# A gated recurrence and a highway layer: another order of all operations, with the first load of f_logit ahead of the first of x

## The chip, the cores and the metric

The kernel runs on one core of a Trainium2 chip. The metric is the device time of one execution in microseconds (us); the times shown are medians of several executions. A profiled execution stands beside them: its own time, and the span that the profile covers, which is a little shorter. The engines are called PE (TensorE; PEld is its weight load), DVE (VectorE), ACT (ScalarE), POOL (GpSimd) and SP (SyncE, which issues the DMAs here).

## The reference

```python
sig = 1.0 / (1.0 + np.exp(-f_logit))                 # x, f_logit: 4 x 6336 x 256, float32
f = lower_bound + (1.0 - lower_bound) * sig
i = 1.0 - f
for t in range(S):                                   # S = 6336, for each of 4 sequences
    h = f[:, t] * h + i[:, t] * x[:, t]
    y[:, t] = h
# then, over all 25344 tokens of y
H = np.maximum(y @ w_h, 0.0)                         # w_h, w_t: 256 x 256
T = 1.0 / (1.0 + np.exp(-(y @ w_t + b_t)))
out = T * H + (1.0 - T) * y
```

## The kernel before

The 25344 tokens are cut into 29 units of 2, 2, 4, 4, 4, then 22 times 8, 4 and 2 blocks of 128 tokens (`parts`, L42). A unit is loaded with tokens on the partitions, turned so that the 256 channels lie on the partitions as two halves of 128, scanned along time, multiplied by both weights, and turned back by two matmuls that also add the parts of the result.

Every step of a unit is one token of the string `order` (L49): a letter, the unit, the half or piece, a `v` if the step runs on DVE instead of its usual engine, and behind the colon the number of its buffer. The tokens are issued in the order of the string, and `pin` keeps that order on each engine; nothing else plans the work. The letters are:

| token | what | engine | line |
|---|---|---|---|
| l, x | load of f_logit, of x (1024 KB for a unit of 8 blocks) | SP | L253 |
| u | u = sigmoid(-f_logit) | ACT | L265 |
| b | bv = u * x, by halves | POOL, or DVE with v | L273 |
| i, p | transposes of u and of bv | PE | L281, L301 |
| f | f = 1 - c * u from the transposed u | ACT, or DVE with v | L292, L290 |
| s | the scan along time, result y | DVE | L320 |
| z, g | the products with w_t and w_h | PE | L332, L112 |
| t | t = sigmoid(z + b_t) | ACT | L345 |
| d | d = max of -c * y and g (the weight w_h has one subtracted on its diagonal) | DVE | L349 |
| e | d * t, in pieces | POOL, or DVE with v | L355 |
| o | turned back, sum of c * y and d * t | PE | L377, L378 |
| c | copy from PSUM to SBUF | ACT, or DVE with v | L390, L388 |
| w | store | SP | L394 |

The two-letter tokens prepare constants once: wh and wt load the weights, pc and pb turn lower_bound and b_t, cc and cb store them, dg makes a diagonal matrix, IW subtracts one from the diagonal of w_h (POOL, L209), WHa and WTa scale the weights (ACT, L225). A token `k*N:slot` takes a PSUM buffer and fills it with N matmuls of zeros whose result nobody reads (`busy`, L120; L123 and L112 in the profile); with N = 0 it only takes the buffer. Three more zero matmuls (L151) always stand ahead of the string.

DVE and POOL products are tied by the helper `shared`: a POOL product waits for the last DVE product ahead of it in the string, if there is one that no POOL product has waited for yet.

There are six buffers for l and x each, eight for bv and y, four for u and f, three for t and d, five for the output, and in PSUM three double banks (slots 0 to 2) beside two single ones for transposes (a0 and a1, which other steps use too).

Of the kernel before, what the change touches and what calls it, by code (L numbers as in the profile page):

```python
# [61 lines left out]
c6.0:0 z8.1:1 i10.0:0 t8.1:2 s9.0:2 x11:5 f10.0v:0 e6.2 u11:3 g8.1:2 p9.1:1 z8.0:0 e7.2 i10.1:0 e7.0 l16:1 t8.0 g8.0:1 w3.0 o6.1:0
f10.1:2 d8.1:2 l12:2 s9.1:3 d8.0 e8.2v i11.0:0 k*2:2 u13:0 p10.1:1 s10.1:4 g9.1:2 c6.1:3 w5.1 w6.0 f11.0:1 e8.1 o7.0:1 c7.0:4 z9.0:0
l14:3 d9.1:1 t9.0:1 i13.1:0 p10.0:1 g9.0:1 f13.1:3 e8.0 s10.0:5 b11.0:6 z9.1:2 o7.1:0 p11.0:0 i11.1:1 d9.0 u12:1 b11.1:7 t9.1 o8.1:1
g10.0:2 f11.1:2 s11.0:0 d10.0:0 x12:0 c7.1:1 i12.1:1 w5.0 e9.0 x13:1 c8.1:0 u16:2 p11.1:0 f12.1v:0 b12.1:0 z10.0:0 t10.0:0 z10.1:1
o8.0:2 s11.1:1 t10.1 i12.0:1 b12.0:1 b13.0:3 l15:4 g10.1:0 f12.0:1 x14:2 w6.1 u14:3 i13.0:0 p12.1:1 w8.1 f13.0:2 c8.0v:2 x15:3 d10.1
g11.0:1 z11.0:2 z11.1:0 s12.1:6 d11.0:2 t11.0:2 p12.0:0 i14.0:1 b13.1:4 g11.1:2 k*1:1 o9.1:1 w7.0 t11.1 f14.0:0 p13.0:1 e10.0 s12.0:7
d11.1 o9.0:0 u15:1 w8.0 c9.1:3 i14.1:0 z12.0:2 f14.1:1 g12.1:1 x16:4 l18:5 i15.0:0 c9.0:0 s13.0:2 d12.1:1 b14.0:2 p13.1:1 o10.0:0
s13.1:3 w9.1 w7.1 f15.0:2 b14.1:5 b16.1:6 z12.1:1 t12.0:1 i16.0:0 l17:0 b15.0:7 o10.1:2 c10.0:4 t12.1 g13.0:0 c10.1:2 p14.0:1 z13.0:1
g12.0:2 f16.0:3 t13.0:0 e11.0v d13.0:0 s14.0:4 d12.0 z13.1:0 p14.1:0 w10.0 u18:0 l20:2 t13.1 s14.1:5 i15.1:1 f15.1:0 w9.0 w10.1 x17:5  # L70
o11.0:1 o11.1:2 b15.1:0 g13.1:0 e12.0 d13.1 p15.1:1 c11.1:3 i18.0:0 c11.0:1 s15.1:0 z14.0:2 f18.0:1 t14.0:2 z14.1:0 b16.0:1 t14.1
p15.0:0 o12.1:1 i16.1:1 g14.1:2 e13.0 o12.0:0 s15.0:1 d14.1:2 p16.0:0 u17:3 s16.0:6 l19:1 w11.1 f16.1:0 c12.1:4 c12.0:0 u20:1 g14.0:2
z15.1:1 d14.0 w11.0 x18:0 x19:1 t15.1:1 w12.1 i17.0:1 p16.1:0 s16.1:7 f17.0:2 g15.1:0 o13.1:2 o13.0:1 b17.0:3 i18.1:1 x20:2 d15.1:1
c13.1:2 p17.0:0 s17.0:2 c13.0:3 f18.1:3 z15.0:2 g15.0:0 l21:3 e14.0 b17.1:4 t15.0 i17.1:1 x21:3 d15.0 g16.0:1 z16.0:2 p17.1:0 d16.0:0
b18.1:2 f17.1:0 z16.1:0 u19:2 s17.1:3 g16.1:1 i19.0:1 b18.0:5 t16.0:0 d16.1 e15.0v t16.1 o14.0:2 f19.0:2 e16.0v c14.0:1 i19.1:0 o14.1:0
c14.1:4 z17.0:1 p18.0:1 w13.0 f19.1:0 w13.1 w12.0 s18.0:4 z17.1:2 b20.1:0 b19.0:7 b19.1:1 g17.1:0 t17.0:2 i20.0:0 t17.1 u21:3 o16.1:1
l22:4 p18.1:1 d17.1:2 g17.0:2 f20.0:1 o16.0:0 w14.0 b20.0:6 s18.1:5 c16.1:3 d17.0 l23:5 b21.1:3 i21.1:0 p19.0:1 f21.1:3 z18.0:1 k*0:2
p19.1:0 c16.0:2 s19.0:6 z18.1:2 o15.0:0 w16.1 t18.0:1 g18.1:1 t18.1 c15.0:0 x22:4 s19.1:7 e17.0 u22:0 p20.0:1 d18.1:0 o15.1:2 i21.0:0
g18.0:0 z19.0:1 s20.0:0 c15.1:1 f21.0:2 w16.0 d18.0 g19.0:2 d19.0:1 i20.1:1 p20.1:0 z19.1:0 t19.0:0 b21.0:4 f20.1:0 t19.1 o17.0:1
s20.1:1 e18.0 g19.1:2 l24:0 c17.0:3 d19.1 u23:2 b22.0:5 b22.1:2 o17.1:0 p21.0:1 i22.1:0 w17.0 w14.1 z20.1:1 s21.0:2 g20.1:2 f22.1:1  # L80
c17.1:2 p21.1:0 i22.0:1 t20.1:2 d20.1:2 f22.0:0 s21.1:3 o18.1:0 c18.1:3 o18.0:1 g20.0:2 p22.1:1 u24:1 x23:5 d20.0 s22.1:4 g21.0:0
i23.0:0 z21.0:2 c18.0:4 l28:2 e19.0 f23.0:2 w17.1 z20.0:1 i23.1:0 p22.0:1 d21.0:0 t21.0:1 f23.1:3 b23.1:7 w15.0 b23.0:1 l25:1 x24:0
t20.0 g21.1:2 e20.0 o19.0:0 u28:3 s22.0:5 i24.0:0 c19.0:2 o19.1:1 f24.0:1 p23.1:1 d21.1 w15.1 c19.1:0 z21.1:0 g22.1:2 s23.1:6 w18.1
t21.1 b24.0:6 z22.1:1 p23.0:0 o20.0:0 u25:0 d22.1:1 c20.0:1 t22.1:0 g22.0:2 s23.0:7 l26:3 i24.1:1 x25:1 o20.1:0 d22.0 p24.0:0 f24.1:0
b24.1:0 c20.1:3 z22.0:1 i25.0:1 t22.0 s24.0:0 g23.0:2 f25.0:3 w19.0 z23.1:0 p24.1:0 d23.0:2 g23.1:1 e21.0 o21.1:2 t23.1:2 b25.0:4
i25.1:1 u26:2 s24.1:1 o21.0:0 f25.1:2 c21.1:2 w20.0 p25.0:0 b25.1:3 x26:2 l27:4 d23.1 s25.0:2 c21.0:1 g24.1:1 w20.1 i28.1:1 z24.1:2
e23.2 e22.1 d24.1:0 z24.0:0 f28.1:1 p25.1:1 i26.0:0 w21.1 e22.0v t24.1:1 e22.2v e23.1v t24.0 f26.0:0 z23.0:2 s25.1:3 o22.0:1 b26.0:2
i28.0:0 o22.1:0 w18.0 t23.0 g24.0:2 f28.0:3 e23.0v c22.0:3 b26.1:5 e24.2 i26.1:0 w22.0 g25.0:1 d24.0 c22.1:2 u27:1 d25.0:1 f26.1:2
p26.0:1 o23.0:0 x27:3 z25.0:2 c23.0:4 w22.1 s26.0:4 e24.0 p26.1:0 w23.0 o23.1:1 z25.1:0 t25.0:0 c23.1:3 g25.1:2 t25.1 i27.0:1 s26.1:5
# [345 lines left out]
```

## Time and profile before

| | |
|---|---|
| median of 3 runs | 206.47 us (206.3 to 208.65) |
| profiled execution | 205.65 us, its span 203.9 us |
| busy, share of the span | PE 92%, DVE 94%, ACT 95%, POOL 85% |
| DMA | 78.68 MB, mean 386 GB/s |

A row of the table by stage gives a stretch of the span, its length, and the busy time of PE, PEld, DVE, ACT and POOL in it with the number of instructions, then TensorE's granted clock, the DMA engines' mean share and the GB/s. A row of a group by shape gives line, engine, operation, what is written and read, the count, the busy time in us, the mean of one in ns, and the idle time of the engine just ahead of them with what ended it. A row of the timeline gives start, length and the instruction, with the idle time ahead of it in brackets. A row of the chain of waits gives start, length and what the chain went through. A row of the waits gives who waited for whom: us in total, how often, the longest.

### The profile page before, as it was taken

The page shows a single profiled execution, that of the slowest core. Times are in us where ns is not written, and L with a number is a line of the kernel's source. Part 1 is how long each engine was busy: PE and PEld are TensorE (multiplying, and loading weights), DVE is VectorE, ACT ScalarE, POOL GpSimd, SP SyncE. Part 2 cuts the span into 40 slices and gives each one's busy share as a digit, 9 for nine tenths or more (in the row PEclk, how much of TensorE's full clock was granted, in tenths as well). Part 3 has the DMA queues.
Part 4 walks back from the last instruction along what each step waited for, and adds up shares of the span by engine and source line. Part 5 has one row for each costly group of instructions (what it writes and reads, how often), then busy time and mean ns, then how long its engine had stood idle before and what let it go on. Part 6 is the DMA issues. An engine that isn't in the chain of part 4 may idle for free.

```text
span 203.9 us, 4594 instructions
## 1 busy us (share of the span) xinstructions
PE 187.5 (92%) x1794; PEld 131.9 (65%) x1820; DVE 192.6 (94%) x162; ACT 194.2 (95%) x203; POOL 172.8 (85%) x96
## 2 busy tenths in 40 slices
...
GB/s 213 367 420 424 416 418 423 409 420 422 418 426 416 423 424 417 420 419 424 417 423 420 427 416 416 427 419 273 336 341 411 420 416 399 209 289 367 272 372 251
DMA packets 16413, 78.68 MB, mean 386 GB/s; under 512 B 1796, under 2 KB 2568, under 8 KB 10760
## 3 DMA queue, kind: packets, MB, share of 16 engines
...
q10 hardware_dynamic: 8, 0.00, 0.0%
...
## 4 chain that ended last, share of the span: by engine, by line
PE 47%; POOL 13%; ACT 12%; DMA 11%; DVE 7%; issue 5%; SPq 1%; ACTq 0%; POOLq 0%; DVEq 0%
DMA x<-in_x_dram 11%; POOL bv L273 8%; PE op L377 7%; PE op L378 7%; PE z L332 6%; PE g L332 6%; PE uT L281 6%; POOL d L355 6%; PE bT L301 5%; DVE y L320 5%; PE z L112 5%; PE g L112 5%; ACT o L390 4%; ACT t L345 3%; ACT f L292 3%
## 5 line engine op out<-in xcount | busy, mean ns | idle before, releaser
L273 POOL TENSOR_TENSOR bv<-u,x 128x1024 bf16<-128x1024 f16 (+2 forms) x53 | 103.7, 1981 | 15.9 <-DVE d L355 7.7
L320 DVE TENSOR_TENSOR_SCAN y<-f,y,bT 128x1024 bf16<-128x1024 f16 (+5 forms) x56 | 107.4, 1929 | 1.1 <-ACT f L292 0.9
L355 POOL TENSOR_TENSOR d<-d,t 128x512 bf16<-128x512 bf16 (+3 forms) x30 | 68.1, 2279 | 6.3 <-ACT t L345 3.6
L349 DVE SCALAR_TENSOR_TENSOR d<-y,ncc,g 128x1024 bf16<-128x1024 bf16 (+2 forms) x58 | 63.6, 1107 | 0.4 <-issue 0.2
L345 ACT ACTIVATE t<-z,bt 128x1024 bf16<-128x1024 f32 (+2 forms) x58 | 58.5, 1048 | 0.5 <-PE z L112 0.5
L292 ACT ACTIVATE f<-uT,ncc 128x1024 f16<-128x1024 f16 (+2 forms) x55 | 58.1, 1060 | 0.5 <-PE uT L281 0.2
L390 ACT COPY o<-op 128x1024 f32<-128x1024 f32 (+2 forms) x55 | 50.9, 966 | 2.1 <-PE op L378 1.8
L265 ACT ACTIVATE u<-l 128x2048 f16<-128x2048 f32 (+2 forms) x29 | 50.4, 1736 | 1.8 <-DMA l<-in_f_logit_dram 1.7
L378 PE MATMUL op<-ident_b,d 128*128 128x128 bf16 x396 | 49.7, 219 | 1.2 <-DVE d L355 0.9
L377 PE MATMUL op<-diag,y 128*128 128x128 f16 x396 | 50.0, 219 | 0.8 <-DVE d L349 0.3
L378 PEld LDWEIGHTS <-d 128*128 128x128 bf16 x396 | 44.0, 113 | 5.5 <-issue 1.3
L377 PEld LDWEIGHTS <-y 128*128 128x128 bf16 x396 | 44.2, 113 | 2.4
L332 PE MATMUL z<-y,w_sb 128*128 128x512 bf16 (+1 forms) x116 | 39.7, 368 | 0.7 <-DVE d L349 0.2
L332 PE MATMUL g<-y,w_sb 128*128 128x512 bf16 (+1 forms) x112 | 39.3, 367 | 1.0 <-DVE d L349 0.2
L301 PE MATMUL bT<-ident_f,bv 128*128 128x128 f32 x198 | 31.9, 277 | 4.8 <-POOL bv L273 2.3
L281 PE MATMUL uT<-ident_h,u 128*128 128x128 f16 x396 | 31.5, 219 | 2.9 <-DVE y L320 1.5
L281 PEld LDWEIGHTS <-u 128*128 128x128 f16 x396 | 26.5, 98 | 11.8 <-issue 4.7
L332 PEld LDWEIGHTS <-w_sb 128*128 128x128 f16 x232 | 22.2, 98 | 14.8 <-ACT f L292 0.2
L301 PEld LDWEIGHTS bT<-ident_f,bv 128*128 128x128 f32 x198 | 22.6, 141 | 14.1 <-POOL bv L273 5.8
L112 PE MATMUL z<-y,w_sb 128*128 128x512 bf16 x79 | 29.9, 379 | 0.0
L112 PE MATMUL g<-y,w_sb 128*128 128x512 bf16 x76 | 28.8, 379 | 0.1
L112 PEld LDWEIGHTS <-w_sb 128*128 128x128 f16 x176 | 17.2, 98 | 15.2 <-issue 1.4
...
## 6 DMA issues: line engine op xcount, KB each, us to landing
...
x<-in_x_dram SPq DMA_DIRECT2D x22, 1024.0 KB, 15.0
...
out_dram<-o SPq DMA_DIRECT2D x2, 256.0 KB, 15.0
```

What stands on the lines that cost most here:

```text
L112: return pe.add_instruction(mybir.InstMatmult(name=nc.get_next_instruction_name(), start_tensor_calc=start, stop_tensor_calc=stop, tile_si ...
L273: shared(pin(e.tensor_mul(bv[:, :nb // 2].rearrange("p k d j -> p k j d"), st[n]["u"][:, :nb, own].rearrange("p (k j) d -> p k j d", j=2), ...
L281: pin(nc.tensor.transpose(uT[:, j * P:(j + 1) * P], st[n]["u"][:, j, h * P:(h + 1) * P], ident_h))
L292: pin(nc.scalar.activation(to, of, AF.Identity, scale=ncc[:, h:h + 1], bias=1.0))
L301: pin(nc.tensor.transpose(words[:, k:k + g * (P - 1) + 1:g], pair, ident_f))
L320: pin(nc.vector.tensor_tensor_scan(y[:, c:e], st[n]["f", h][:, c:e], st[n]["bT", h][:, c:e], 0.0 if fresh else carry[h], op0=ALU.mult, op1 ...
L332: pin(nc.tensor.matmul(p[:, a:e], w, half(n, "y", ki)[:, a:e], start=ki == 0, stop=ki == NH - 1))
L345: pin(nc.scalar.activation(half(n, "t", m), st[n]["z", m][:, :tokens(n)], AF.Sigmoid, bias=bt[:, m:m + 1]))
L349: pin(nc.vector.scalar_tensor_tensor(half(n, "d", m), half(n, "y", m), ncc[:, m:m + 1], st[n]["g", m][:, :tokens(n)], op0=ALU.mult, op1=AL ...
L355: shared(pin(e.tensor_mul(st[n]["d"][:, a:c], st[n]["d"][:, a:c], st[n]["t"][:, a:c])), not eng)
L377: pin(nc.tensor.matmul(o, half(n, "y", h)[:, cols], diag[:, h], start=True, stop=False))
L378: pin(nc.tensor.matmul(o, half(n, "d", h)[:, cols], ident_b, start=False, stop=True))
```

## The change

Only the string `order` is replaced. Both strings have 850 tokens and the same units, pieces and loads; what differs is their order, the buffers' numbers, which of the b, f, e and c run on DVE, and the fillers. The first load is now l0, ahead of x0. Loads of the start, before: x0 l0 l1 wh x1 l2 wt x2 l3 x3; after: l0 x0 l1 wh x1 wt l2 x2 l3 x3. The fillers by tokens are 21 matmuls of zeros before and 15 after.

On DVE before: b0.1 b0.0 b1.1 b1.0 b2.1; f1.0 f10.0 f12.1; e0.1 e0.0 e1.1 e1.0 e2.0 e3.1 e4.0 e6.0 e6.1 e8.2 e11.0 e15.0 e16.0 e22.0 e22.2 e23.1 e23.0 e24.1 e25.1 e26.2 e26.0 e27.1 e27.0 e28.0; c8.0 c27.1. On DVE after: b0.1 b2.0; f0.1 f1.1 f6.1 f8.0 f17.1; e2.0 e6.0 e7.0 e9.0 e8.0 e13.0 e16.0 e19.0 e23.0 e22.0 e25.0 e26.0 e26.2 e27.1 e28.0 e28.1; c27.0 c28.0 c28.1.

The beginning and the end of both strings (the rest, as far as the counts go, is summed up above):

```diff
-k*3:a0 x0:0 pc:0 l0:0 l1:1 cc u0:0 k*3:1 pb:2 i0.0:1 k*4:0 dg wh u1:1 b0.1v:0 f0.0:0 b0.0v:1 i1.0:0 x1:1 l2:2 wt IW f1.0v:1 p0.0:1 WHa
-cb i0.1:0 s0.0:0 f0.1:2 x2:2 b1.1v:2 b1.0v:3 k*2:1 i1.1:1 k*1:0 p0.1:0 f1.1:3 p1.0:1 s0.1:1 k*1:2 p1.1:0 l3:3 g0.0:1 s1.0:2 g0.1:0 u2:2
-s1.1:3 x3:3 k*1:2 i2.1:1 d0.1:0 l4:4 WTa d0.0 g1.0:2 i2.0:0 g1.1:0 z1.1:1 b2.1v:4 f2.1:0 d1.1:1 d1.0 f2.0:2 p2.1:1 s2.1:4 b2.0:5 t1.1:0
-z0.0:1 z0.1:0 z1.0:2 u3:3 x4:4 t0.1:1 t1.0 t0.0 l5:5 x5:5 p2.0:0 b3.1:6 i3.1:1 f3.1:1 s2.0:5 e0.1v e0.0v e1.1v k*3:0 i3.0:0 g2.0:2 l6:0
-u4:0 e1.0v x6:0 b3.0:7 z2.0:1 b4.0:1 f3.0:3 p3.1:1 t2.0:2 d2.0:2 g2.1:0 i4.1:0 o0.0:2 z2.1:1 f4.1:0 s3.1:6 b4.1:0 d2.1 c0.0:0 t2.1
-p3.0:1 i4.0:0 f4.0:2 s3.0:7 e2.0v p4.0:0 l7:1 z3.1:2 x7:1 p4.1:1 o1.0:0 s4.0:0 u5:1 c1.0:1 s4.1:1 z3.0:1 i5.1:0 g3.1:0 e2.1 t3.0:1
-g4.1:1 d3.1:0 i5.0:1 g3.0:0 d4.1:1 b5.1:3 b5.0:2 f5.1:1 t3.1 p5.1:0 l8:2 f5.0:3 z4.0:2 z4.1:1 u6:2 t4.0:0 p5.0:1 d3.0 o2.0:0 l9:3
-s5.1:2 t4.1 s5.0:3 e3.0 c2.0:2 b6.1:4 i6.1:0 b6.0:5 g4.0:2 f6.1:2 e4.1 u7:3 p6.1:1 z5.1:1 i6.0:0 d4.0 z5.0:0 s6.1:4 g5.0:2 t5.1:2
-f6.0:0 p6.0:1 i7.0:0 x8:2 l10:4 e3.1v e4.0v g5.1:1 d5.0:2 o4.0:2 w1.0 s6.0:5 i7.1:1 t5.0 b7.0:6 x9:3 d5.1 f7.0:1 u8:0 c4.0:3 p7.0:0
-e5.0 s7.0:0 g6.0:0 b7.1:7 f7.1:3 g6.1:1 d6.1:1 p7.1:1 e5.2 i8.1:0 u9:1 x10:4 z6.0:2 f8.1:2 t6.0:1 z6.1:1 t6.1 i8.0:0 o3.0:2 f8.0:0
-b8.1:1 s7.1:1 u10:2 g7.0:1 b8.0:0 p8.0:1 d6.0 l11:5 e6.0v e6.1v w2.0 i9.0:0 d7.0:0 o5.1:0 w0.0 c3.0:4 b9.0:3 s8.0:6 e5.1 z7.1:1 f9.0:1
-b10.1:2 g7.1:2 p8.1:0 i9.1:1 l13:0 b9.1:4 t7.1:0 c5.1:1 z7.0:1 d7.1 f9.1:3 w4.0 o5.0:2 e7.1 p9.0:1 o6.0:0 s8.1:7 b10.0:5 t7.0 c5.0:2
 ...
-w24.0 c25.2 o25.1:2 z27.1:1 c25.0:1 p28.0:1 g27.1:a0 t27.1:1 c25.1 b28.1:0 e26.2v e26.0v e26.1 o26.2:0 s28.0:0 z27.0:1 w25.1 d27.1:0
-p28.1:1 o26.3:2 c26.2:2 g27.0:a0 o26.1:0 s28.1:1 t27.0 e27.1v c26.3 g28.1:1 d27.0 c26.1:0 o26.0:2 e27.0v z28.1:a1 z28.0:0 c26.0
-o27.1:a0 d28.1:1 w25.0 o27.0:1 w26.1 c27.1v:4 w26.0 g28.0:2 t28.0:0 t28.1 e28.1 d28.0 e28.0v o28.1:a1 c27.0 w27.0 c28.1:3 o28.0:a0
-w28.1 c28.0:1 w28.0
+l0:0 k*3:a0 k*0:0 pc:1 k*0:2 u0:0 i0.0:1 x0:0 l1:1 cc wh i0.1:0 b0.1v:0 x1:1 b0.0:1 dg f0.0:0 p0.1:1 f0.1v:1 IW u1:1 b1.1:2 s0.1:0 WHa
+k*2:0 p0.0:0 wt s0.0:1 k*4:2 i1.1:1 pb:1 WTa f1.1v:2 l2:2 k*0:0 g0.0:2 i1.0:0 f1.0:3 x2:2 g0.1:0 p1.1:1 d0.0:0 l3:3 b1.0:3 p1.0:0 d0.1
+z0.0:2 z0.1:0 u2:2 cb s1.1:2 t0.0:0 k*1:1 s1.0:3 b2.0v:4 i2.0:1 x3:3 i2.1:0 f2.0:1 b2.1:5 g1.0:1 e0.0 t0.1 f2.1:0 p2.0:1 s2.0:4 z1.1:2
+z1.0:0 p2.1:0 l4:4 u3:3 x4:4 b3.0:6 s2.1:5 e0.1 b3.1:7 l5:5 d1.0:1 k*2:a1 t1.1:1 g1.1:2 d1.1 t1.0 i3.0:1 f3.0:2 p3.0:0 x5:5 z2.0:0
+s3.0:6 i3.1:1 u4:0 z2.1:1 g2.0:2 f3.1:3 t2.1:2 i4.1:0 p3.1:1 b4.1:0 d2.0:2 f4.1:1 o0.0:1 g2.1:2 i4.0:0 t2.0 l6:0 e1.0 s3.1:7 b4.0:1
+p4.1:1 u5:1 d2.1 z3.1:0 g3.0:2 s4.1:0 f4.0:0 p4.0:1 e1.1 i5.0:0 t3.1:0 x6:0 c0.0:0 d3.0:0 o1.0:2 l7:1 e2.1 b5.0:2 s4.0:1 g3.1:0 d3.1
+i5.1:1 g4.0:1 f5.0:2 e2.0v b5.1:3 d4.0:1 z3.0:0 c1.0:1 f5.1:3 t3.0 p5.0:0 x7:1 l9:2 o2.0:2 k*1:1 u6:2 c2.0:2 s5.0:2 g4.1:0 p5.1:1
+s5.1:3 i6.0:0 z4.0:1 f6.0:1 e3.1 l8:3 d4.1 t4.0:1 w0.0 z4.1:2 i6.1:0 t4.1 b6.1:4 p6.1:1 z5.1:1 x8:2 g5.1:0 l10:4 f6.1v:0 u7:3 t5.1:2
+i7.0:0 f7.0:2 b6.0:5 s6.1:4 z5.0:2 k*1:1 x9:3 d5.1:2 l11:5 w1.0 p6.0:1 i7.1:0 e3.0 e4.1 t5.0 b7.1:6 e5.2 f7.1:3 u9:0 s6.0:5 g5.0:1
+p7.1:0 o3.0:0 i9.0:1 z6.0:2 d5.0 b7.0:7 g6.1:1 c3.0:3 e4.0 f9.0:0 s7.1:6 d6.1:0 u8:1 p7.0:1 g6.0:0 i8.1:0 e5.0 t6.0:0 o4.0:1 s7.0:7
+f8.1:1 o5.1:2 i8.0:0 d6.0 l12:0 f8.0v:3 i9.1:1 e5.1 b8.1:0 g7.1:0 u10:2 c5.1:4 c4.0:0 p8.1:0 f9.1:2 x12:4 b8.0:1 z6.1:2 g7.0:1 t6.1
+b9.0:2 p8.0:1 u11:3 o5.0:2 d7.1:1 c5.0:1 b9.1:3 s8.1:0 z7.1:0 i11.0:0 x10:5 s8.0:1 d7.0 t7.1:1 e6.2 p9.0:1 w2.0 w5.1 f11.0:1 s9.0:2
 ...
+t26.1:0 g26.0:1 c24.0:3 w24.1 t26.0 b28.0:6 o25.3:2 b28.1:1 w21.0 d26.0 e26.0v c25.3:1 o25.2:a0 i28.1:1 e26.2v c25.2 f28.1:1 w22.1
+o25.0:0 o25.1:2 c25.0:0 z27.1:a0 p28.0:1 e26.1 s28.0:0 g27.0:1 z27.0:0 d27.0:0 c25.1 t27.1:2 o26.3:2 w24.0 p28.1:1 s28.1:1 g27.1:a0
+o26.2:1 d27.1 t27.0 o26.1:0 c26.3:4 c26.2 e27.0 w25.1 e27.1v c26.1:2 g28.0:2 o26.0:a1 w25.0 c26.0 z28.0:1 o27.0:a0 z28.1:0 d28.0:1
+t28.0:1 w26.1 o27.1:2 g28.1:1 c27.0v:3 e28.0v t28.1 d28.1 w26.0 e28.1v o28.0:0 c28.0v:1 o28.1:a1 c27.1 c28.1v:0 w27.0 w28.0 w28.1
```

More of the change, by code (lines that the diff above doesn't have):

```diff
@@ L62 @@
[L62 to L89, printed above, removed]
@@ L90 @@
-d25.1 e25.0 o24.1:1 e24.1v g26.1:0 i27.1:0 d26.1:2 b27.0:7 g26.0:2 c24.1:2 f27.1:0 b27.1:1 z26.1:1 x28:4 d26.0 f27.0:2 p27.0:0 w23.1
-z26.0:0 t26.1:2 w21.0 e25.2 w24.1 o24.0:2 p27.1:1 o25.3:1 s27.0:6 e25.1v o25.2:a0 t26.0 b28.0:6 s27.1:7 c24.0:4 o25.0:0 c25.3:3 w19.1
-w24.0 c25.2 o25.1:2 z27.1:1 c25.0:1 p28.0:1 g27.1:a0 t27.1:1 c25.1 b28.1:0 e26.2v e26.0v e26.1 o26.2:0 s28.0:0 z27.0:1 w25.1 d27.1:0
-p28.1:1 o26.3:2 c26.2:2 g27.0:a0 o26.1:0 s28.1:1 t27.0 e27.1v c26.3 g28.1:1 d27.0 c26.1:0 o26.0:2 e27.0v z28.1:a1 z28.0:0 c26.0
@@ new lines @@
+b9.0:2 p8.0:1 u11:3 o5.0:2 d7.1:1 c5.0:1 b9.1:3 s8.1:0 z7.1:0 i11.0:0 x10:5 s8.0:1 d7.0 t7.1:1 e6.2 p9.0:1 w2.0 w5.1 f11.0:1 s9.0:2
+e7.2 e6.1 l13:1 z7.0:2 t7.0 e6.0v b10.0:4 z8.0:0 b10.1:5 t8.0:2 i10.0:0 z8.1:1 t8.1 p9.1:1 o6.1:2 g8.0:0 x11:0 e7.0v f10.0:3 w4.0
+g8.1:1 w5.0 c6.1:2 p10.0:0 s9.1:3 u12:1 i10.1:1 x13:1 f10.1:0 d8.1:2 b12.1:6 d8.0 o6.0:2 s10.0:4 c6.0:4 z9.0:1 e7.1 g9.1:0 l14:2
+b11.1:7 b11.0:0 p10.1:1 d9.1:0 w3.0 s10.1:5 u13:0 t9.0:0 b12.0:1 o7.1:2 i11.1:0 o7.0:0 w6.0 f11.1:2 c7.0:0 g9.0:1 d9.0 i12.0:0 c7.1:1
@@ new lines @@
+p11.1:1 z9.1:0 f12.0:3 s11.1:6 z10.0:2 t9.1 i12.1:0 e9.0v z10.1:1 e8.0v i13.1:1 w6.1 t10.0:1 g10.0:0 e8.1 t10.1 f13.1:0 d10.0:1 g10.1:2
+f12.1:2 o9.0:1 e8.2 b13.1:2 d10.1 p11.0:1 o8.0:0 p12.1:0 c9.0:3 x14:2 l18:3 e10.0 o8.1:2 u14:2 l15:4 w7.1 s11.0:7 s12.1:0 g11.1:1
+c8.1:4 c8.0:2 i13.0:1 b13.0:3 w7.0 w9.0 b14.1:4 f13.0:1 z11.1:2 p12.0:0 t11.1:0 d11.1:2 b14.0:5 g11.0:0 i14.1:1 o9.1:1 s12.0:1 z11.0:2
+u18:3 p13.1:0 d11.0 f14.1:2 p13.0:1 t11.0 s13.1:2 z12.0:0 x15:3 c9.1:1 t12.0:2 o10.0:2 z12.1:1 l16:5 c10.0:0 u15:1 w8.0 w8.1 g12.1:0
```

22 lines of the change are left out of this document (added).

## The prediction

> **What bounds the kernel now.** I read the page's totals first, then the table by stage, then the chain of waits, then the timelines of the first 50 us, then the groups kept apart by shape.
>
> ```profile
> span 203.9 us, 4594 instructions
> PE 187.5 (92%) x1794; PEld 131.9 (65%) x1820; DVE 192.6 (94%) x162; ACT 194.2 (95%) x203; POOL 172.8 (85%) x96
> 0.00:20.00 20.00, 16.19 (x102) 8.71 (x104) 15.05 (x32) 16.32 (x28) 8.21 (x18) 1.00 0.92 354
> 20.00:60.00 40.00, 35.80 (x341) 24.91 (x345) 39.21 (x31) 39.86 (x38) 37.34 (x22) 1.00 1.02 419
> ...
> 140.00:180.00 40.00, 39.35 (x398) 28.57 (x402) 39.69 (x28) 40.00 (x40) 37.93 (x16) 1.00 0.87 339
> 180.00:204.00 24.00, 19.13 (x215) 14.63 (x215) 18.93 (x23) 18.09 (x27) 13.12 (x11) 0.97 0.84 320
> ```
>
> Columns of the stage rows: length, busy time of PE, PEld, DVE, ACT, POOL, granted clock, DMA share, GB/s. From 20 to 180 us DVE and ACT have no idle time to speak of (39.21 and 39.86 of 40, then 39.69 and 40.00), and until 140 us DMA is full as well. The idle time that an order could win back lies at the two ends: 5.0 us of DVE and 3.7 us of ACT before 20 us, 5.1 and 5.9 us after 180 us. Even all of DVE's idle time, 203.9 - 192.6 = 11.3 us, is only 5.5% of the span, and the first load's latency and the last store keep most of it.
>
> ```profile
> 0.74 0.38 SPq L253 DMA_DIRECT2D x<-in_x_dram  x1
> 1.18 0.90 SPq L253 DMA_DIRECT2D l<-in_f_logit_dram  x2
> 4.13 0.63 ACT L265 ACTIVATE u<-l 128x512 f16<-128x512 f32 x1 [1.29 <-DMA l<-in_f_logit_dram]
> 10.59 16.55 DMA x<-in_x_dram
> 27.28 2.15 POOL bv L273
> 30.23 2.35 DVE y L320
> ```
>
> The first three rows are the timeline: x0 is issued at 0.74 us, l0 at 1.18, and u0 starts at 4.13 when l0 is there. The other three are the chain of waits: to 27.1 us (10.59 + 16.55) it runs through an x transfer, then through POOL's product of u and x (by POOL's list, in which IW, b2.0, b3.1, b3.0, b4.0, b4.1, e2.1, b5.1, b5.0 and e3.0 come first, this is b6.1, so the transfer is x6), then through the scan of unit 6. So the start is bound by the load stream, not by what the engines do with it, and from 30 us on by DVE and ACT, with POOL close behind.
>
> **The change part by part.** Both orders hold the same 850 tokens but for slots, fillers and engines, so the work can be counted. Engines first: durations by shape.
>
> ```profile
> L273 POOL TENSOR_TENSOR bv<-u,x 128x1024 bf16<-128x1024 f16 x44 | 94.4, 2169 | 7.8 <-DVE d L355 5.1 <-ACT t L345 1.4 <-DMA x<-in_x_dram 0.8
> L273 POOL TENSOR_TENSOR bv<-u,x 128x512 bf16<-128x512 f16 x7 | 8.0, 1167 | 7.6 <-DVE bv L273 5.0 <-DVE d L355 2.1 <-DMA x<-in_x_dram 0.4
> L273 POOL TENSOR_TENSOR bv<-u,x 128x256 bf16<-128x256 f16 x2 | 1.3, 687 | 0.5 <-DVE d L355 0.5
> L273 DVE TENSOR_TENSOR bv<-u,x 128x256 bf16<-128x256 f16 x4 | 1.5, 439 | 0.0
> L355 POOL TENSOR_TENSOR d<-d,t 128x2048 bf16<-128x2048 bf16 x10 | 40.8, 4078 | 0.3 <-POOL bv L273 0.3
> L355 POOL TENSOR_TENSOR d<-d,t 128x1024 bf16<-128x1024 bf16 x5 | 10.6, 2137 | 0.0
> L355 POOL TENSOR_TENSOR d<-d,t 128x512 bf16<-128x512 bf16 x14 | 16.1, 1159 | 2.4 <-DVE d L355 2.4
> L355 POOL TENSOR_TENSOR d<-d,t 128x256 bf16<-128x256 bf16 x1 | 0.7, 667 | 3.6 <-ACT t L345 3.6
> L355 DVE TENSOR_TENSOR d<-d,t 128x2048 bf16<-128x2048 bf16 x3 | 3.6, 1215 | 0.0
> L355 DVE TENSOR_TENSOR d<-d,t 128x1024 bf16<-128x1024 bf16 x4 | 2.7, 681 | 0.1
> L355 DVE TENSOR_TENSOR d<-d,t 128x512 bf16<-128x512 bf16 x12 | 4.9, 426 | 0.1
> L355 DVE TENSOR_TENSOR d<-d,t 128x256 bf16<-128x256 bf16 x5 | 1.2, 282 | 0.1
> L209 POOL TENSOR_TENSOR w_raw<-w_raw,ident_f 128x128 f32<-128x128 f32 x2 | 0.9, 453 | 3.5 <-DMA w_raw<-in_moe_w_h_dram 3.5
> L290 DVE TENSOR_SCALAR f<-uT,ncc 128x1024 f16<-128x1024 f16 x2 | 2.5, 1267 | 0.0
> L290 DVE TENSOR_SCALAR f<-uT,ncc 128x256 f16<-128x256 f16 x1 | 0.5, 485 | 0.8 <-PE uT L281 0.8
> L292 ACT ACTIVATE f<-uT,ncc 128x1024 f16<-128x1024 f16 x42 | 50.4, 1200 | 0.0
> L390 ACT COPY o<-op 128x1024 f32<-128x1024 f32 x42 | 44.2, 1091 | 0.9 <-PE op L378 0.8
> L390 ACT COPY o<-op 128x256 f32<-128x256 f32 x2 | 0.6, 375 | 0.9 <-PE op L378 0.9
> L388 DVE COPY o<-op 128x1024 f32<-128x1024 f32 x1 | 1.2, 1194 | 0.0
> ```
>
> *DVE.* Three b of 256 leave it: -1.32. Its e go from 24 (5, 12, 4, 3 of 256, 512, 1024, 2048) to 16 (2, 3, 7, 4): 12.89 to 11.47, -1.42. Its f go from two of 1024 and one of 256 to three and two: +1.75. Of its copies one of 1024 and one of 512 become one of 512 and two of 256; a copy of 256 on DVE isn't shown, so I take ACT's 0.375 (bounds 0 and 1.194): -0.44. Sum -1.4 us.
> *ACT.* One f of 1024 and one of 256 less (the latter at DVE's 0.485; ACT's own lies between that and nothing shorter is shown), one copy of 1024 more, two of 256 less: -1.20 - 0.49 + 1.09 - 0.75 = -1.35 us.
> *POOL.* Three b of 256 more (+2.06); its e go from 30 (1, 14, 5, 10) to 38 (4, 23, 2, 9): 68.4 to 70.3. Sum +4.0 us, to about 177 of 204.
> *PE.* Fifteen zero matmuls by slots instead of 21; PE's idle time is not on the chain at either end, so 0.
>
> So the two full engines each lose about 1.4 us over the whole run. How much of it reaches the end depends on where it lies, and there the x6 transfer cuts the run in two.
>
> *Before x6 (to 27.3 us).* With l0 ahead of x0, l0 is issued 0.44 us earlier (1.18 - 0.74) and u0 can start that much earlier; bounds 0 (l0's latency may not shrink) and 1.29 (ACT's whole wait). wt moves ahead of l2, which puts 256 KB before l2 (0.6 us at 419 GB/s); x2 keeps its place. But up to x6 stand the same transfers in both orders: x0 to x6, l0 to l6 and both weights (256 KB each for units 0 and 1 and the weights, 512 for 2 to 4, 1024 for 5 and 6: 8.9 MB). So x6 lands at 27.1 us again, and the 0.44 us ends in the wait for it. What it costs if that cover is gone: up to 0.44 us gained.
>
> What can go wrong there is POOL. Before b6.1 its list now has 17 operations instead of 10 (b0.0, b1.1, b1.0, e0.0, e0.1, e1.0, e1.1 are the new ones): 18.1 us instead of 13.4 by the rows above (IW is the two at L209). The first four fit into the time when it idled (the first row below: 5.05 us). From b2.1 on, which can start at about 11.5 us as POOL's first b did at 11.66, 15.2 us remain; operations overlap a little, and the window's row below has 17.03 us busy for nine operations of 17.47 us by their means, so 14.8: POOL is through at 26.3 us, 1.0 us ahead of x6, if it waits for nothing. It will wait: for x3 as now, and for e2.0 on DVE, which stands ahead of b5.1 (the helper `shared` lets a POOL operation wait for the DVE product before it).
>
> ```profile
> POOL bv L273 <- DVE d L355: 7.7, 7, 2.6
> POOL d L355 <- DVE d L355: 2.4, 3, 1.0
> 27.28:45.06 17.78, 14.77 (x126) 9.46 (x126) 17.02 (x12) 17.64 (x16) 17.03 (x9) 1.00 1.01 417
> 11.66 1.17 POOL L273 TENSOR_TENSOR bv<-u,x 128x512 bf16<-128x512 f16 x1 [5.05 <-DVE bv L273]
> 40.80 4.26 POOL L273 TENSOR_TENSOR bv<-u,x 128x1024 bf16<-128x1024 f16 x2
> 47.21 2.34 DVE L320 TENSOR_TENSOR_SCAN y<-f,y,bT 128x1024 bf16<-128x1024 f16 x1
> ```
>
> Ten such waits took 10.1 us, 1.0 each. With 1.0 for e2.0 and 0.4 for x3 (the row of b of 512), b6.1 starts at 27.7 instead of 27.3: **+0.4 us**; bounds 0 (no wait) and +1.5 (the 2.1 + 0.4 us that the b of 512 waited).
>
> *Units 6 to 8.* From b6.1 to the end of b8 POOL had nine operations, 17.47 us by their means; now it has twelve (e3.0, e4.0 and e5.1 are added), 20.95, and times 17.03/17.47 that is 20.4 us. From 27.3 the last b8 would end at 47.7 and the one ahead of it at 45.6 us. Between the end of b6.1 (29.43) and its scan (30.23) lie 0.8 us of transposes, so s8.1 could start at 46.4. DVE, by its own list, has four products less from s6.1 up to there (e3.1, e4.0 and e6.1 of 512, e6.0 of 1024: 1.96) and f8.0 more (1.27); that stretch took 47.21 - 30.23 = 16.98 and now takes 16.3, so DVE is there at 46.5. That fits with nothing to spare, where the old order had b8 done at 45.06, 2.2 us ahead of its first scan. Bounds of the wait: 0 and 3.5 (all of POOL's added work); nearest to 0, because no DVE product stands inside this list, but with no slack I take **+0.3 us**.
>
> *From the first scan of unit 6 to the end* DVE has 0.7 us less. Of its -1.4 us, the other 0.7 lie ahead of s6.1: three b and four e of 256 and f1.0 gone (1.32 + 1.13 + 0.49), f0.1, f1.1 and f6.1 added (0.97 + 1.27). **-0.7 us.** POOL then gains slack again, because the new order gives DVE whole products of 2048 or pieces of 1024 from unit 6 on. The load order later keeps or lengthens the distance from issue to use, so no new DMA wait: 0. At the tail the last product, the last two copies and three stores follow each other in the same way, both copies on DVE instead of ACT: 0, bounds -0.3 (one copy's 0.375) and +0.4.
>
> Sum: +0.4 + 0.3 - 0.7 = 0.0 us. The profiled execution took 205.65 us with a span of 203.9; the median of the runs shown is 206.47. I take 0.1 off for the 0.44 us at the start (a quarter of it) and forecast **206.3 us**, a span of about 203.8.
>
> **The rivals.**
> *A. POOL becomes the bound and it ends slower.* If b6.1 starts 1.5 us late and POOL waits in units 6 to 11 as much as it did between 20 and 60 us, where it idled 40 - 37.34 = 2.66 us, then with no slack all of it reaches DVE: 1.5 + 2.66 - 0.7 = +3.5, some 209.8 us. It decides when POOL's idle time between 12 and 50 us is over about 1.5 us. For it: the +8.2 us of POOL work up to b8 (18.1 + 20.95 against 13.4 + 17.47). Against: three DVE products ahead of b8 instead of twelve, so fewer of the 1.0 us waits. Two such waits more and it passes 210.6.
> *B. The lighter engines gain.* If x6 isn't what holds b6.1 (its transfer may land sooner where the stream starts smoother), DVE's and ACT's 1.4 us and the 0.44 us count in full and nothing is lost at unit 8: -1.8, 204.6 us. For it: ACT, 40.00 of 40, gets 1.35 us less. Against: x6 has the same bytes ahead.
> *C. PE runs slow at first.* The new order has no filler between lbT's transpose and the first transposes of u.
>
> ```profile
> 1.19 1.46 PE L151 MATMUL idle<-zeros 128*128 128x512 bf16 x3 [1.19 <-DVE zeros L148]
> 4.41 0.59 PE L112 MATMUL idle<-zeros 128*128 128x512 bf16 x2
> ```
>
> Three zero matmuls took 1.46 us at the start, two took 0.59 at 4.41: the pace doubles at about 4 us. If it stays slow some us longer, each of the four groups in a row ahead of e0 (transposes of u and b, g, z) costs 0.49 - 0.30 = 0.19 us more, 0.8 in all; POOL reaches b6.1 that much later, and the time is 207.1. [...]
> *D. The start doesn't move:* u0 waits for something other than its place in the queue, and the 0.1 goes: 206.4.
>
> **How the numbers follow.** Forecast with D: 0.50 (205.3 to 207.3). A: 0.27, of it 0.11 beyond 210.6. B: 0.16, of it 0.05 beyond -2% (202.3), where the tail's 5 us of idle time would have to shrink as well. C: 0.07. A measurement of this kernel tells about 2%, 4.1 us, from no change. So faster 0.05, same 0.84, slower 0.11. The range leaves out the upper end of A and the lower end of B: 203.9 to 210.2.
>
> **What would show it.** Right: b6.1 at 27 to 28 us after a wait for x; u0 at 3.7; DVE over 39 of 40 from 20 to 60 us with POOL over 38.5. Wrong: gaps of DVE in front of scans of units 6 to 11 that end with POOL's b (A); x6 landing before 26 us, or DVE under 190.5 us busy with no new idle time (B); zero matmuls still at 0.42 us apart after 5 us (C). It would be wrong as a whole if a wait deep in the new order (a scan behind its f on ACT, a store that holds a load) cost more than any at the start, which the counts can't exclude.

## The result: 0.7% slower, and where the time went

The changed kernel took 208.36 us (median of 20 executions, 205.66 to 211.5), the kernel before 206.47 us (20 executions, 205.82 to 208.65). The ratio is 1.0071 with a 95% interval of 1.0049 to 1.0094; it isn't the quotient of the two medians, since disturbed executions, some 3 to 4 us longer, are left out of it and of the ratios below. The profiled execution took 208.23 us, its span 206.4.

First the totals of the changed kernel's page, then its table by stage (length; busy PE, PEld, DVE, ACT, POOL; granted clock, DMA share, GB/s). Its `order` has one line less, so every line number is smaller by one: L354 is now the product e.

```profile
span 206.4 us, 4642 instructions
PE 190.2 (92%) x1814; PEld 131.5 (64%) x1814; DVE 195.1 (95%) x154; ACT 193.8 (94%) x200; POOL 177.3 (86%) x107
```

```profile
0.00:20.00 20.00, 16.66 (x97) 8.87 (x98) 13.31 (x25) 15.09 (x25) 12.17 (x25) 1.00 0.93 354
20.00:60.00 40.00, 36.48 (x333) 23.94 (x332) 39.60 (x30) 40.00 (x39) 38.32 (x24) 1.00 1.01 417
...
140.00:180.00 40.00, 38.42 (x383) 27.48 (x382) 40.00 (x28) 39.18 (x38) 36.42 (x16) 1.00 0.89 360
180.00:204.00 24.00, 22.32 (x244) 16.55 (x241) 22.52 (x25) 20.60 (x30) 16.72 (x14) 1.00 0.71 272
```

Two things catch the eye. DVE was busy for only 13.31 of the first 20 us instead of 15.05, which is a larger drop than the 0.7 us by which its list ahead of unit 6 had been counted lighter; and over the whole run it was busy for 195.1 us instead of 192.6, though 1.4 us had been taken from it. The groups by shape say which product grew, and the timelines of DVE and POOL say why.

```profile
L354 DVE TENSOR_TENSOR d<-d,t 128x2048 bf16<-128x2048 bf16 x4 | 8.2, 2044 | 0.0
L354 DVE TENSOR_TENSOR d<-d,t 128x1024 bf16<-128x1024 bf16 x7 | 4.6, 679 | 0.1
```

```profile
106.60 2.95 DVE L354 TENSOR_TENSOR d<-d,t 128x2048 bf16<-128x2048 bf16 x1
130.07 1.20 DVE L354 TENSOR_TENSOR d<-d,t 128x2048 bf16<-128x2048 bf16 x1
148.38 2.83 DVE L354 TENSOR_TENSOR d<-d,t 128x2048 bf16<-128x2048 bf16 x1
```

```profile
100.00 8.47 POOL L272 TENSOR_TENSOR bv<-u,x 128x1024 bf16<-128x1024 f16 x4
109.72 2.17 POOL L272 TENSOR_TENSOR bv<-u,x 128x1024 bf16<-128x1024 f16 x1 [1.25 <-DVE d L354]
...
143.74 11.59 POOL L272 TENSOR_TENSOR bv<-u,x 128x1024 bf16<-128x1024 f16 x5
```

The mean of a DVE product of 2048 went from 1215 to 2044 ns, that of 1024 stayed at 0.68 us. Two of the four took 1.20 us and two far longer: e13.0 (106.60) and e19.0 (148.38). When e13.0 was issued, the last of POOL's four b ran until 108.47 (100.00 + 8.47), and e13.0 ended 1.08 us after that. So it was not computing for 2.95 us: b17.0 still took 1.87 us when e13.0 was issued, and e13.0 took 1.75 us longer than the 1.20 us of an undisturbed one. e19.0 came 0.4 us after the start of b22.0 and took about 1.6 us longer. In the kernel before, by contrast, POOL had reached its wait when DVE came to its large products:

```profile
120.30 2.36 DVE L355 TENSOR_TENSOR d<-d,t 128x2048 bf16<-128x2048 bf16 x2
122.79 10.60 POOL L273 TENSOR_TENSOR bv<-u,x 128x1024 bf16<-128x1024 f16 x5 [2.62 <-DVE d L355]
```

There two products took 2.36 us together, and POOL paid with 2.62 us of idle time. POOL loses time at an overlap as well: five of its products took 10.60 us there, and 11.59 us from 143.74 on in the changed kernel, where b22.1, issued while e19.0 was at work, took 3.15 us instead of 2.2.

The other loss is at the start (first ACT's row of u1 in the kernel before, then rows of ACT, PE, DVE and POOL in the changed kernel):

```profile
4.95 0.63 ACT L265 ACTIVATE u<-l 128x512 f16<-128x512 f32 x1 [0.19 <-DMA l<-in_f_logit_dram]
...
3.57 0.63 ACT L264 ACTIVATE u<-l 128x512 f16<-128x512 f32 x1 [0.71 <-DMA l<-in_f_logit_dram]
5.99 0.63 ACT L264 ACTIVATE u<-l 128x512 f16<-128x512 f32 x1 [0.83 <-DMA l<-in_f_logit_dram]
6.98 1.49 PE L111 MATMUL idle<-zeros 128*128 128x512 bf16 x3
8.71 0.48 DVE L289 TENSOR_SCALAR f<-uT,ncc 128x256 f16<-128x256 f16 x1 [1.17 <-PE uT L280]
12.75 1.28 DVE L319 TENSOR_TENSOR_SCAN y<-f,y,bT 128x512 bf16<-128x512 f16 x1 [0.71 <-PE bT L300]
27.61 4.25 POOL L272 TENSOR_TENSOR bv<-u,x 128x1024 bf16<-128x1024 f16 x2
31.76 2.35 DVE L319 TENSOR_TENSOR_SCAN y<-f,y,bT 128x1024 bf16<-128x1024 f16 x1
47.95 4.58 DVE L319 TENSOR_TENSOR_SCAN y<-f,y,bT 128x1024 bf16<-128x1024 f16 x2
```

u0 starts 0.56 us earlier (3.57 against 4.13), but u1 a whole microsecond later (5.99 against 4.95). At 7 us zero matmuls still run at the slow pace (three in 1.49 us), DVE waits 1.17 and 0.71 us for transposes, and the first scan of unit 6 starts at 31.76 instead of 30.23. POOL's b6.1, at 27.61, isn't what it waited for: it took 2.15 us and its transposes 0.8, and DVE was still busy when they were done.

### The profile page after: what moved, and what is told of

It is laid out like the page before. It is cut to its first block, busy times and chain, and to the rows that moved or that the text cites. A ratio compares the mean times of both kernels' runs of the same rounds, so it can differ in the third digit from the quotient of the medians.

```text
span 206.4 us, 4642 instructions
## 1 busy us (share of the span) xinstructions
PE 190.2 (92%) x1814; PEld 131.5 (64%) x1814; DVE 195.1 (95%) x154; ACT 193.8 (94%) x200; POOL 177.3 (86%) x107
## 5 line engine op out<-in xcount | busy, mean ns | idle before, releaser
L272 POOL TENSOR_TENSOR bv<-u,x 128x1024 bf16<-128x1024 f16 (+2 forms) x56 | 106.8, 1931 | 13.8 <-DVE bv L272 5.8
L354 POOL TENSOR_TENSOR d<-d,t 128x512 bf16<-128x512 bf16 (+3 forms) x38 | 69.9, 1850 | 6.5 <-DVE d L354 2.1
L291 ACT ACTIVATE f<-uT,ncc 128x1024 f16<-128x1024 f16 (+2 forms) x53 | 54.9, 1045 | 1.6 <-PE uT L280 1.4
L389 ACT COPY o<-op 128x1024 f32<-128x1024 f32 (+1 forms) x54 | 50.8, 974 | 1.6 <-PE op L377 1.2
L264 ACT ACTIVATE u<-l 128x2048 f16<-128x2048 f32 (+2 forms) x29 | 49.1, 1693 | 1.7 <-DMA l<-in_f_logit_dram 1.7
L331 PE MATMUL g<-y,w_sb 128*128 128x512 bf16 (+1 forms) x116 | 40.3, 368 | 0.9 <-DVE d L348 0.5
L300 PE MATMUL bT<-ident_f,bv 128*128 128x128 f32 x198 | 32.4, 279 | 5.0 <-DVE y L319 2.6
L111 PE MATMUL z<-y,w_sb 128*128 128x512 bf16 x88 | 33.3, 379 | 0.0
L111 PE MATMUL g<-y,w_sb 128*128 128x512 bf16 x88 | 33.3, 379 | 0.0
```

The costliest lines, as they stand in the source:

```text
L111: return pe.add_instruction(mybir.InstMatmult(name=nc.get_next_instruction_name(), start_tensor_calc=start, stop_tensor_calc=stop, tile_si ...
L272: shared(pin(e.tensor_mul(bv[:, :nb // 2].rearrange("p k d j -> p k j d"), st[n]["u"][:, :nb, own].rearrange("p (k j) d -> p k j d", j=2), ...
L291: pin(nc.scalar.activation(to, of, AF.Identity, scale=ncc[:, h:h + 1], bias=1.0))
L300: pin(nc.tensor.transpose(words[:, k:k + g * (P - 1) + 1:g], pair, ident_f))
L331: pin(nc.tensor.matmul(p[:, a:e], w, half(n, "y", ki)[:, a:e], start=ki == 0, stop=ki == NH - 1))
L354: shared(pin(e.tensor_mul(st[n]["d"][:, a:c], st[n]["d"][:, a:c], st[n]["t"][:, a:c])), not eng)
```

## The experiments

**1. Take the two holds away.** Theory H: a POOL product that runs holds a DVE product of two SBUF operands. The edit changes only which of the two stands first in POOL's view; DVE's order is the same.

```diff
-s15.0:7 b17.0:3 i16.0:1 ... o12.1:0 e13.0v p16.0:0
+s15.0:7 i16.0:1 ... o12.1:0 e13.0v b17.0:3 p16.0:0
-o18.1:1 b22.0:2 b22.1:7 ... i23.1:0 e19.0v
+o18.1:1 e19.0v b22.0:2 b22.1:7 ... i23.1:0
```

> The changed kernel with two POOL products put behind the DVE products that they overlapped: b17.0 behind e13.0, and e19.0 ahead of b22.0; DVE's own order is the same. Theory H (a running POOL product holds a DVE product of two SBUF operands until it ends; this cost 1.75 + 1.65 us in the profile of the changed kernel): both DVE products take 1.2 us again instead of 2.95 and 2.83, DVE busy falls from 195.1 to about 191.7 us, and the time from about 208.2 to 205 to 206 us, as far as DVE sets the end. Rival A (POOL's added work is the bound): POOL now waits 1 to 2 us twice and the time stays at 208 us or rises.

205.95 us; ratio to the kernel before 0.9972 (0.9956 to 0.9989). DVE's timeline of this kernel has e13.0, e16.0 and e19.0:

```profile
106.92 1.20 DVE L354 TENSOR_TENSOR d<-d,t 128x2048 bf16<-128x2048 bf16 x1
128.63 1.52 DVE L354 TENSOR_TENSOR d<-d,t 128x2048 bf16<-128x2048 bf16 x1
147.27 1.21 DVE L354 TENSOR_TENSOR d<-d,t 128x2048 bf16<-128x2048 bf16 x1
```

e13.0 and e19.0 are back at 1.2 us, and 2.4 us of the median are gone (1.0% by the two ratios, 1.0071 and 0.9972). POOL now waits, 1.55 us ahead of b17.0 and 1.72 us ahead of b22.0, and the time falls all the same. (e16.0 now meets the end of b20.1 and is held for 0.3 us.)

**2. Only the first of the two moves.**

```diff
-s15.0:7 b17.0:3 i16.0:1 ... o12.1:0 e13.0v p16.0:0
+s15.0:7 i16.0:1 ... o12.1:0 e13.0v b17.0:3 p16.0:0
```

> The changed kernel with only the first of the two moves: b17.0 behind e13.0. Theory H counts the holds one by one: e13.0 takes 1.2 us, e19.0 still 2.8, and half of the first experiment's gain comes, so about 207.0 us. If the gain of the first experiment came from something else (another order of POOL from unit 22 on, say), the time is at one of the two ends, 205.95 or 208.3 us.

206.91 us, ratio 1.0026 (1.0011 to 1.0040): 1.45 us of the 2.4 in the medians, and by the ratios 0.45% of 1.0%. In its one profile, of an execution of 209.76 us, e13.0 took 1.20 and e19.0 2.82 us, as expected. So the holds count one by one, each for about half; the second was not taken away alone.

**3. Put a hold in**, into the kernel of experiment 1.

```diff
-i12.1:0 e9.0v z10.1:1 e8.0v ... e8.2 b13.1:2
+i12.1:0 b13.1:2 e9.0v z10.1:1 e8.0v ... e8.2
```

> The first experiment's kernel (no long hold left) with one put in on purpose: b13.1 of POOL ahead of e9.0 of DVE, where POOL waited for e9.0 and e8.0 from 71.2 to 73.3 us. Theory H: e9.0, which starts at 71.3, takes about 3.2 us instead of 1.2, and the time rises from 205.95 by 1.5 to 2.0 to about 207.7 us, though POOL has its product 2 us earlier and its own wait shrinks. If the holds cost only what POOL's order makes later (rival A), the time stays at 206 or falls.

207.59 us, ratio 1.0077 (1.0056 to 1.0098): 1.64 us more than without in the medians, and 1.05%, some 2.2 us, by the two ratios. Rows of DVE in this kernel; the second holds e9.0 and e8.0:

```profile
69.05 2.34 DVE L319 TENSOR_TENSOR_SCAN y<-f,y,bT 128x1024 bf16<-128x1024 f16 x1
71.31 3.67 DVE L354 TENSOR_TENSOR d<-d,t 128x2048 bf16<-128x2048 bf16 x2
74.91 1.27 DVE L348 SCALAR_TENSOR_TENSOR d<-y,ncc,g 128x1024 bf16<-128x1024 bf16 x1
```

In the changed kernel the same two took 1.80 us. POOL had its product earlier, and it was no use. Rival A fell.

**4. Put a hold into the kernel before.**

```diff
-b18.0:5 t16.0:0 d16.1 e15.0v t16.1 ... z17.1:2 b20.1:0 b19.0:7
+b18.0:5 t16.0:0 d16.1 b20.1:0 e15.0v t16.1 ... z17.1:2 b19.0:7
```

> The kernel before with one POOL product (b20.1) put ahead of e15.0, so that it runs when DVE comes to e15.0; POOL waited 2.62 us at that place. Theory H: e15.0 takes about 3.2 us instead of 1.22, POOL's wait of 2.62 us shrinks to about 2.5 for the next one or less, and the time rises by 1.5 to 2.0 us to 208.2 us. If such an overlap is no hold, e15.0 keeps 1.2 us, POOL gains 2 us and the time stays at 206.4 us.

208.63 us, ratio 1.0097 (1.0068 to 1.0126): +2.2 us in the medians, a little over the 1.5 to 2.0 expected. In its one profile, of an execution of 211.57 us, e15.0 and e16.0 took 3.40 us instead of 2.36, and e11.0, which the edit doesn't touch, 5.37 us instead of 1.20 beside two POOL products in a row. So an overlap of this kind costs time in the old order too, but that the 2.2 us are the price of the one hold put in is argued from the times, not shown.

**5. The fillers at the start out.** Theory S: the zero matmuls ahead of unit 1's transposes are what delays DVE.

```diff
-k*2:0 p0.0:0 wt s0.0:1 k*4:2 i1.1:1
+k*0:0 p0.0:0 wt s0.0:1 k*0:2 i1.1:1
```

> The changed kernel without the six zero matmuls that stand ahead of p0.0 and i1.1 (k*2 and k*4 become k*0). Theory S (these matmuls, run at the slow pace of 0.43 us each, delay the transposes of unit 1 and so f1.1 on DVE, which waited 1.17 us for them; DVE then reaches the first scan of unit 6 at 31.8 us instead of 30.2): i1.1 at 6.7 instead of 8.3 us, the first scan of unit 6 0.7 to 1.2 us earlier, the time 207.2 us. Rival C (the slow pace itself is what costs, and less filling keeps it longer): the first scan of unit 6 at 31.8 or later, 208.2 us or more. By a third view (unit 6 waits for x6 or for POOL) nothing moves. The holds of 1.7 us each may stay or move.

209.63 us, ratio 1.0153 (1.0127 to 1.0179): slower still. Theory S fell. Rows of PE and DVE in this kernel:

```profile
10.76 1.06 PE L331 MATMUL z<-y,w_sb 128*128 128x256 bf16 x4
12.04 1.06 PE L280 MATMUL uT<-ident_h,u 128*128 128x128 f16 x8
33.01 2.35 DVE L319 TENSOR_TENSOR_SCAN y<-f,y,bT 128x1024 bf16<-128x1024 f16 x1
```

f1.1 did start earlier (6.83 us), but PE stayed at the slow pace: eight transposes took 1.06 us at 12 us, where eight took 0.61 us in the kernel before at 21 us. The first scan of unit 6 came at 33.0. The largest part of the delay is DVE's wait for the transposes of b2.0, ahead of the first scan of unit 2: 1.52 us here, 0.71 in the changed kernel.

**6. Both edits together** (1 and 5).

> Both edits of the two kernels ahead together. If H and S hold and DVE sets the end, the gains add: 3.4 + 1.0 us off 208.2, so 204 to 205 us, below the kernel before (206.4). If one of them only uncovers the next bound (ACT was busy 194 us in both kernels), 205.5 to 206.5 us.

206.56 us, ratio 1.0010 (0.9989 to 1.0031): above the first guess and at the end of the second; its median is 0.6 us above that of experiment 1 alone (ratio 0.9972, 0.9956 to 0.9989), and the two intervals just touch, so leaving the fillers out probably costs time here too. Where is not shown: in its profile the first scan of unit 6 came at 32.09, as in experiment 1 (32.08).

**7. The pauses filled instead**, on top of experiment 1.

```diff
-l0:0 k*3:a0 k*0:0 pc:1 k*0:2 u0:0 i0.0:1 ... i0.1:0 b0.1v:0
+l0:0 k*3:a0 k*0:0 pc:1 k*2:2 u0:0 i0.0:1 ... i0.1:0 k*2:2 b0.1v:0
```

> The first experiment's kernel (two POOL products put behind) with zero matmuls in PE's two early pauses: two after lbT's transpose and two after the transposes of unit 0's u. Theory C (PE kept its slow pace of 0.43 us per zero matmul until 8.5 us and beyond, since its work paused between 4 and 5 us, and DVE waited 2.6 us for transposes there): the pace doubles between 4.3 and 6 us, f1.1 starts 0.5 to 1 us earlier, the first scan of unit 6 at 31.0 to 31.5 instead of 32.1, the time 205.0 to 205.4 us instead of 205.95. Rival (the added matmuls stand in the way of the transposes, as fillers do): 205.9 us or more.

205.40 us, ratio 0.9964 (0.9945 to 0.9982). PE's and DVE's rows:

```profile
4.46 0.63 PE L111 MATMUL idle<-zeros 128*128 128x512 bf16 x1
5.54 0.38 PE L111 MATMUL idle<-zeros 128*128 128x512 bf16 x1
6.79 0.81 PE L111 MATMUL idle<-zeros 128*128 128x512 bf16 x3
31.40 2.35 DVE L319 TENSOR_TENSOR_SCAN y<-f,y,bT 128x1024 bf16<-128x1024 f16 x1
```

The pace doubled between 4.5 and 5.5 us, three fillers took 0.81 us, and the first scan of unit 6 came at 31.40 instead of 32.08. The gain of 0.55 us in the median fits, but the two ratios' intervals overlap: it is likely, not shown. That the filled pauses are the cause is not shown either: in experiment 8, whose pauses are not filled, the pace doubled as early. This is the fastest version tried, 0.36% below the kernel before.

**8. x0 first again**, on top of experiment 1.

```diff
-l0:0 k*3:a0 k*0:0 pc:1 k*0:2 u0:0 i0.0:1 x0:0 l1:1
+x0:0 l0:0 k*3:a0 k*0:0 pc:1 k*0:2 u0:0 i0.0:1 l1:1
```

> The first experiment's kernel with x0 issued first again, ahead of l0. Theory L: u0 at 4.1, u1 at 4.9 instead of 5.6, the first scan of unit 6 up to 0.7 us earlier, 205.3 us. By the change's own aim (an earlier u0 is worth something) it is up to 0.5 us slower, 206.4 us. If neither matters ahead of the wait for x6, 205.95 us.

206.06 us, ratio 0.9985 (0.9971 to 1.0): no difference from 205.95. u0 went back to 4.17 us; u1 started at 5.63 and not at 4.9, now behind f0.0 on ACT and not waiting for its load, so this run doesn't show when l1 landed. PE's and DVE's rows:

```profile
4.85 0.40 PE L280 MATMUL uT<-ident_h,u 128*128 128x128 f16 x4 [0.73 <-ACT u L264]
6.63 0.81 PE L111 MATMUL idle<-zeros 128*128 128x512 bf16 x3
31.50 2.35 DVE L319 TENSOR_TENSOR_SCAN y<-f,y,bT 128x1024 bf16<-128x1024 f16 x1
```

They bear on theory C of experiment 7. Here nothing fills PE's pauses, and PE waited 0.73 us ahead of the transposes of unit 0, yet these four already took 0.40 us (0.61 in experiment 1) and the three fillers 0.81. The first scan of unit 6 came at 31.50, nearly as early as with the pauses filled. So pauses of this length don't by themselves keep the pace slow, and why it stayed slow in experiment 1 is open.

**9. The kernel before with l0 first**, the title's edit by itself.

```diff
-k*3:a0 x0:0 pc:0 l0:0 l1:1
+l0:0 k*3:a0 x0:0 pc:0 l1:1
```

> The kernel before with l0 issued ahead of x0 and nothing else. By the prediction's step (the 0.44 us end in the wait for x6) u0 starts at about 3.6 instead of 4.13 us and the time stays at 206.4 us within 0.3. Theory L (the swap makes l1 land later: u1 started at 5.6 to 6.0 us in every run of the new order, and at 4.9 in the old one): u1 at 5.6 or later here too, DVE's first scan of unit 6 later by up to 0.7 us, the time up to 207.1 us.

206.72 us, ratio 1.0025 (0.9997 to 1.0053): no gain, perhaps a small loss. ACT's two rows and DVE's scan of unit 6:

```profile
3.47 0.63 ACT L264 ACTIVATE u<-l 128x512 f16<-128x512 f32 x1 [0.63 <-DMA l<-in_f_logit_dram]
5.91 0.63 ACT L264 ACTIVATE u<-l 128x512 f16<-128x512 f32 x1 [1.81 <-DMA l<-in_f_logit_dram]
30.50 2.35 DVE L319 TENSOR_TENSOR_SCAN y<-f,y,bT 128x1024 bf16<-128x1024 f16 x1 [0.23 <-ACT f L291]
```

u0 gains 0.66 us, u1 loses 0.96 to l1's later landing, and unit 6 is 0.27 us later. Theory L holds for the landing in this profile; its price is too small for the times to tell. Why l1, third in the queue in both, lands later is open.

**10. A third move: b20.1 behind e16.0**, on top of experiment 7.

```diff
-w14.0 b20.1:6 w14.1 l22:5 i19.1:1 o15.1:0 c15.0:2 e16.0v p19.0:0
+w14.0 w14.1 l22:5 i19.1:1 o15.1:0 c15.0:2 e16.0v b20.1:6 p19.0:0
```

> The kernel with the filled pauses and, as a third move, b20.1 behind e16.0, which it held for 0.3 us. Theory H: e16.0 takes 1.2 instead of 1.5 us and the time falls by 0.3 to 205.1 us. If that POOL product is needed where it stood (POOL waits about 1 us more), 205.4 us or more.

207.17 us, ratio 1.0052 (1.0033 to 1.0072): 1.8 us slower than experiment 7. The first row is POOL's after the move, then DVE's at the scan that was late, then the stage 120 to 150 us of this kernel:

```profile
129.64 4.27 POOL L272 TENSOR_TENSOR bv<-u,x 128x1024 bf16<-128x1024 f16 x2 [3.12 <-DVE d L354]
...
140.42 2.35 DVE L319 TENSOR_TENSOR_SCAN y<-f,y,bT 128x1024 bf16<-128x1024 f16 x1 [1.89 <-ACT o L389]
...
120.00:150.00 30.00, 27.82 (x284) 20.57 (x287) 28.11 (x19) 28.57 (x28) 25.32 (x11) 1.00 1.02 419
```

e16.0 was no longer held, but POOL stood still for 3.12 us ahead of b20.1, all engines fell behind (DVE 28.11 of 30, against 29.95 in experiment 1) and a scan came 1.89 us late. On the way there, e17.0, third on POOL from b20.1 on, ended at 137.95; PE waited 1.87 us for it inside o17.1, and so came to p20.1, the transposes that this scan needs, only at 139.73; they ended at 140.33. The row names ACT as what ended the wait, but PE's transposes came last. Here a hold of 0.3 us was the cheaper side.

## Why the prediction was wrong, step by step

The forecast was no change, 206.3 us; the kernel is 0.7% slower, which lies inside the range and on rival A's side, but not by rival A's mechanism.

- **b6.1 at 27.7 us** (x6 covers the start, POOL's waits add 0.4): it started at 27.61, so the time was right. It did not come after a wait for x, as the prediction's sign had it, but straight behind e3.1 on POOL: POOL's own list set it.
- **Units 6 to 8** (DVE needs 16.3 us, POOL is just in time, +0.3): DVE took 16.19 (47.95 - 31.76) without a gap. The stretch was right, the +0.3 not needed; POOL's 4 us of added work delayed no scan here, and between 12 and 50 us POOL idled for 0.9 us, not the 1.5 of rival A's condition, so rival A fell. That a late POOL product can delay a scan was shown elsewhere, by experiment 10.
- **DVE at the first scan of unit 6**: the step took for granted that DVE gets there with b6.1, since its list is shorter. It got there 1.53 us later than before. Up to that scan DVE was busy for 24.65 us before and 24.69 after, so that the shorter list saved nothing, and idle for 5.58 and 7.07 us: the whole loss is idle time. The waits are on PE: 0.28, 0.45, 1.17, 0.71 and 0.18 us, 2.8 in all, against 0.77 before (where 0.61 more stood at the scan itself). The prediction had moved work off DVE without asking what DVE's remaining first operations wait for. Part of it is rival C, PE's slow pace, given 0.07 and priced at 0.8 us: in experiments 7 and 8, with the pace doubled early, the wait of 1.17 us was 0.22 and the scan came 0.3 to 0.7 us earlier than in the changed kernel and in experiment 1, but still about 1.2 us later than before. Another part, 0.71 us, stands in the string and was nobody's rival: b2.0 on DVE now comes directly ahead of s2.0, which needs its transposes, where d1.1 and d1.0 stood between b2.1 and s2.1 before; this wait was 0.65 to 0.73 us in experiments 1, 3, 7, 8 and 10 too, whether the pace had doubled at about 5 or at about 9 us. No run changed that place alone. l1's landing may add up to 0.3 (experiment 9); how the rest divides stays open.
- **-0.7 us of DVE work from unit 6 on, from -1.4 over the run**: the failed term. The counts were right, but each large product was priced at 1215 ns, a mean from a kernel in which POOL stood waiting at these very places. In the new order POOL was still running, twice, and DVE's busy time rose by 2.5 us: -1.4, and +3.3 for the four products of 2048 (4 x (2044 - 1215) ns). The remaining 0.6 is about what eight operations fewer can make, an estimate: rows next to each other overlap (two products of 1215 ns took 2.36 us above), so leaving some out saves less than their means add up to. Counted to the last unit's second scan (195.06 us before, 198.05 after), 1.5 us come from the start and 1.5 from this stretch; the tail gave 0.4 back. Without the two holds, in the profile of experiment 1, the stretch took 163.7 us (32.08 to 195.81) against 164.8 before: there the -0.7 came out as -1.1. Experiments 1, 2 and 3 show the holds' price in the medians: 2.4 us for both, 1.45 for one, 1.64 for one put in. "Fewer of the 1.0 us waits", counted in favour of POOL, was the same thing seen from the other side: where POOL didn't wait for DVE's large product, DVE's product took longer (e13.0 and e19.0, 1.75 and about 1.6 us).
- **Without the holds** the new order is at 0.9972 of the old one, -0.6 us; the sum of 0.0 was close to that, in part by luck: in the profile of experiment 1 a start 1.85 us longer, of which the sum had 0.4, stands against gains of 1.1 us in the stretch and 0.4 at the tail.
- **u0 0.44 us earlier, worth 0.1**: u0 came 0.56 us earlier, and neither experiment 8 nor 9 shows a gain from it. As good as right, but l1's later landing was missed.
